# Decay image and constants of the fills: two and four transfers from SP's queue, in a rewritten order, in place of three and six from GpSimd's

## The chip, the core and the metric

The kernel runs on one core of a Trainium2 chip. Its engines work side by side, each on its own list of instructions in order: PE (matrix multiplication, with PEld for its weight loads), DVE (VectorE), ACT (ScalarE), POOL (GpSimd) and SP (SyncE, which here only issues transfers). The metric is device microseconds of one execution, the median of the runs. Times in the text are microseconds from the start of the profiled span unless they say otherwise.

## The reference

A causal attention with a decay ("forgetting") term, followed by a gated feed-forward block with a short convolution. Sizes: 8 batches, 8 heads, 576 positions, 64 columns per head; the feed-forward goes from 512 to 1024 and back.

```
scores = q @ k.T / sqrt(64)
cum    = cumsum(log(clip(f, 1e-4, 1)))            # per batch and head, along the sequence
scores = where(causal, scores + cum[i] - cum[j], -1e9)
x      = softmax(scores) @ v                      # heads side by side: [8, 576, 512]
h      = relu(x @ w_in)                           # [8, 576, 1024]
c      = conv along the sequence, 3 taps per column
out    = (h * sigmoid(c)) @ w_out                 # float32 [8, 576, 512]
```

## The kernel before

**Tiling.** The 64 pairs of batch and head are cut into 16 head blocks (hb) of four heads; two make a batch. The 576 positions are cut into five blocks of keys and queries (four of 128 and one of 64). For a block, q and k stand transposed in one SBUF tile `qk` (a ring of four): 64 rows of each head's data lie at the odd partitions, and the even partitions hold extra rows that the matmul of the scores sums over as well. The decay enters through three of them: on q's side one row holds cum scaled for the queries and two rows hold ones; on k's side one row holds -1 and two rows hold the scaled cum, split in two bf16 parts. Thus `cum[i] - cum[j]` is part of the product, and no other engine adds it.

**How the rows get there.** `kc` (128 x 576, bf16) is made by DVE from a running sum: partitions 0 to 63 the leading part of cum of the 64 heads, 64 to 127 the rest. It is written to a tensor in DRAM, `image`, of four rows (j), two sides (a: q, k), 64 heads and 576 positions; that is task `ki` (`decay_image`, lines 325 to 327). The constants of the image (the ones, the -1 and a zero row on both sides) and a tensor of zeros, `blank`, are written by task `zc` (`constants`, lines 329 to 332). From there three kinds of block read:

- Block 0 takes the decay by extra matmuls from `kc` directly (lines 364 and 366) and reads no image.
- Blocks 1 to 9 (`NCL` = 10) have q and k put in place with one DVE or ACT operation (`cl`) which also writes the constant rows (line 238 for blocks 2 to 9); then `rw` (`rows_of`, lines 254 and 255) brings the three varying rows from the image with two transfers.
- Blocks 10 to 15 are loaded by transfers alone: after the transposing loads, `fi` (`fill`, lines 246 and 248) brings 60 zero rows from `blank` and all four rows of both sides from the image. Only these blocks, heads 40 to 63, use the constants in the image.

**Stages of one head block**, by the names in the order: `q` (transposing load of q or k, line 232; blocks 0 and 1 have plain loads `ld`, line 211, and PE transposes `tp`, line 218, instead), `v` (loads of v, line 261), `va` (cast of v, lines 269 and 271), then per pair of heads `sd` (scores of the diagonal blocks, line 361), `so` (the blocks below it, line 361), per block `st` (the last 64 positions), with the exponentials `ed`, `eo`, `et` on ACT; blocks 0 to 5 mask by a matmul (line 369), the later ones on POOL (`md`, `mt`). Then `pv` (product with v, lines 443 and 447), `n` (division by the sum, line 457), `t` and `tx` (transposition, lines 464 to 474).

**Stages of one batch's feed-forward**, for eight column blocks ff: `f` (line 483, 0.98 us each when PE runs freely), `r` (relu, lines 495 and 497), `c` and `d` (the convolution, lines 502 and 504, DVE), `a` (tanh, line 507, ACT), `g` (gate, line 511, DVE), `k` (copies of the last 64 positions of two batches into one tile, line 516), `o` (line 522), `e` (copy of the result from PSUM) and `s` (store). In the last batch `o7.c.ff` is one matmul of chunk c; chunks 0 and 1 share one PSUM tile, 2 and 3 another, and chunk 4 has its own; their copies are `e7.c` (lines 532 and 537). The weights are loaded in quarters (`wi`, `wo`, line 570) and cast (`wic`, `woc`, line 578).

**What sets the order.** Nothing is scheduled at run time. The string `ORDER` lists every task once; `Plan.play` runs through it and emits each task's instructions, so an engine's list is the order of the tasks that are its own. `name@ENGINE` picks the engine for tasks that several could do. Buffers are handed out in the same order (a task that takes a buffer gets the one freed first), and an engine that comes to an instruction whose inputs or buffer aren't ready waits, with all that stands behind it. Waits are kept per tile: a matmul into one half of a PSUM tile waits for a copy from its other half that stands ahead of it in the order. SP's list therefore is one queue: a transfer that waits for its source holds up all loads behind it.

Of the kernel before, what the change touches and what calls it, by code (L numbers as in the profile page):

```python
# [17 lines left out]
cw dca dcl tb ld0 ld0.0.0 ld0.0.1 ld0.1.0 ld0.1.1 ld1 ld1.0.0 ld1.0.1 v0.0 q2.1 q2.0 wi3@SP cwt dcs dck tp0.0.0  # L18
cl0.0.0@ACT tp0.0.1 tp0.1.0 tp0.1.1 cl0.1.1@DVE cl0.0.1@ACT sd0 cl0.1.0@ACT tp1.0.0 tp1.0.1 tp1.1.0 ed0 cl1.0.0@ACT v0.4
v0.2 cl1.1.0@DVE cl1.0.1@DVE sd1 tp1.1.1 cl1.1.1@ACT ki@POOL st0 rw1 so1.1 so1.0 cl2.1 cl2.0 ed1 eo1.1 et0 eo1.0 so0.1  # L20
sd3 v0.3 v0.1 va1.0@DVE so0.0 wic3@POOL va0.0@POOL va0.1@DVE eo0.1 ed3 q3.1 q3.0 eo0.0 sd2 ed2 so3.0 so2.1 so2.0 eo3.0
eo2.1 pv0.0 st1 so3.1 va1.1@DVE et1 wi0@SP wic0@POOL eo2.0 pv0.1 eo3.1 pv1.0 cl3.1 n0.0 n0.1 rw2 t0 pv1.1 cl3.0 tx0@ACT
sd4 so4.0 wi1@SP rw3 q5.1 n1.0 n1.1 t1 tx1@DVE wi2@SP v1.0 sd5 so5.1 q5.0 ed4 eo4.0 wic1@DVE f0.0 r0.0@DVE c0.0 cl5.1
d0.0 eo5.1 ed5 sd6 q4.0 wic2@POOL f0.1 ed6 so4.1 r0.1@ACT c0.1 v1.2 v1.3 f0.2 f0.3 st3 h0 eo4.1 a0.0 g0.0 d0.1 r0.2@ACT
r0.3@ACT et3 c0.2 c0.3 cl5.0 rw5 v1.1 va2.0@POOL q4.1 so6.1 so5.0 eo5.0 so6.0 eo6.0 sd7 ed7 f0.4 r0.4@ACT zc a0.1 d0.2
c0.4 d0.4 g0.1 f0.5 r0.5@ACT c0.5 d0.3 so7.0 eo7.0 f0.6 st2 et2 eo6.1 v1.4 a0.4 wo2@SP r0.6@DVE sd11 so7.1 so11.0 d0.5
cl4.0 va2.1@POOL wo1@SP g0.4 va3.0@POOL va3.1@POOL ed11 eo7.1 eo11.0 sd10 so10.0 c0.6 eo10.0 f0.7 r0.7@ACT ed10 pv2.0
so11.1 wo3@SP cl4.1 n2.0 d0.6 eo11.1 rw4 a0.2 v2.0 q6.1 pv2.1 so10.1 eo10.1 a0.3 a0.5 a0.6 pv3.0 pv3.1 n2.1 t2 n3.0
tx2@DVE n3.1 c0.7 g0.6 g0.3 d0.7 g0.5 woc2@POOL woc1@POOL sd9 so9.0 t3 ed9 tx3@ACT eo9.0 f1.0 sd8 r1.0@ACT c1.0 a0.7
g0.2 q6.0 cl6.1 d1.0 g0.7 st4 wo0@SP cl6.0 v2.2 so8.1 ed8 et4 eo8.1 f1.1 r1.1@ACT st5 f1.2 v2.4 so9.1 r1.2@ACT f1.3 f1.4  # L30
h1 et5 f1.5 c1.2 v2.3 v2.1 c1.1 a1.0 r1.3@ACT so8.0 rw6 v3.0 v3.1 c1.3 woc0@ACT g1.0 r1.4@ACT woc3@POOL eo9.1 eo8.0 o0.0
d1.3 r1.5@ACT a1.3 d1.1 sd13 sd12 o0.1 ed12 va4.0@DVE c1.4 pv4.0 f1.6 q7.1 q7.0 va5.0@ACT e0.0@ACT va4.1@ACT g1.3 c1.5
d1.4 d1.2 d1.5 ed13 r1.6@ACT pv4.1 n4.0 n4.1 va5.1@ACT a1.5 so13.0 eo13.0 a1.4 a1.1 md13 v3.3 pv5.0 pv5.1 n5.0 n5.1
so12.1 f1.7 q9.1 q9.0 cl7.1 c1.6 g1.1 t4 eo12.1 tx4@ACT v3.2 t5 tx5@ACT r1.7@ACT a1.2 cl7.0 d1.6 a1.6 c1.7 o0.2 k0@POOL
o0.3 rw7 g1.4 g1.2 v3.4 d1.7 v4.0 md12 q8.0 q8.1 e0.1@ACT g1.6 cl9.0 st6 so13.1 et6 eo13.1 f2.0 r2.0@ACT f2.1 c2.0 g1.5
a1.7 r2.1@ACT s0.0@SP f2.2 r2.2@ACT sd15 c2.2 f2.3 so15.1 so12.0 d2.0 g1.7 va6.0@DVE ed15 cl9.1 va7.0@DVE va7.1@DVE c2.1
eo15.1 h2 r2.3@ACT f2.4 sd14 eo12.0 r2.4@ACT ed14 o1.0 a2.0 rw9 q10.1 q10.0 so14.0 st7 so14.1 cl8.0 d2.1 c2.3 g2.0 cl8.1
eo14.1 eo14.0 o1.1 e1.0@ACT va6.1@ACT pv6.0 et7 k1@ACT f2.5 mt7 mt6 r2.5@ACT sd18 pv6.1 n6.0 so15.0 d2.3 a2.1 n6.1
eo15.0 o1.4 md15 md14 ed18 st9 et9 so18.0 t6 d2.2 e1.2@DVE sd19 pv7.0 eo18.0 ed19 c2.4 g2.1 c2.5 tx6@ACT f2.6 so19.1
pv7.1 r2.6@ACT n7.0 n7.1 v4.1 eo19.1 f2.7 so18.1 a2.2 a2.3 eo18.1 rw8 mt9 d2.4 c2.6 md19 d2.5 g2.2 sd16 ed16 a2.5  # L40
r2.7@ACT md18 s0.1@SP d2.6 a2.6 a2.4 v4.2 md16 q11.1 o1.2 t7 tx7@DVE sd17 g2.3 o1.3 v4.4 f3.0 v4.3 ed17 g2.5 c2.7 q11.0
s1.0@SP d2.7 e1.1@ACT r3.0@ACT fi10 so17.0 eo17.0 so16.1 f3.1 r3.1@ACT a2.7 c3.0 g2.4 d3.0 g2.6 f3.2 h3 r3.2@ACT eo16.1
g2.7 f3.3 f3.4 md17 c3.1 r3.3@ACT so19.0 so16.0 r3.4@ACT eo19.0 va9.0@DVE va9.1@ACT eo16.0 so17.1 v5.0 s1.2@SP c3.2 d3.1
c3.3 a3.0 g3.0 fi11 o2.0 f3.5 d3.3 a3.1 eo17.1 st8 r3.5@ACT g3.1 c3.5 va8.0@DVE d3.5 d3.2 c3.4 o2.1 sd20 et8 e2.0@ACT
f3.6 sd21 so20.1 ed20 r3.6@ACT ed21 md21 pv8.0 md20 eo20.1 n8.0 so21.0 v5.3 pv9.0 eo21.0 so21.1 pv9.1 va8.1@POOL mt8
v5.2 q12.0 v5.4 v5.1 n9.0 n9.1 a3.3 g3.3 d3.4 eo21.1 sd23 ed23 md23 pv8.1 n8.1 q12.1 so23.1 eo23.1 f3.7 q13.1 s2.0@SP t9
fi12 r3.7@DVE c3.7 st10 t8 sd22 a3.5 et10 tx8@ACT o2.2 a3.4 ed22 c3.6 tx9@DVE f4.0 mt10 k2@POOL so20.0 o2.3 so22.0 g3.5
va10.0@ACT d3.7 eo20.0 a3.7 pv10.0 r4.0@DVE md22 c4.0 d3.6 a3.2 e2.1@ACT eo22.0 va11.0@DVE g3.4 n10.0 g3.7 a3.6 so22.1
f4.1 f4.2 f4.3 r4.2@ACT g3.6 c4.2 g3.2 d4.0 h4 r4.1@ACT d4.2 f4.4 c4.1 so23.0 r4.3@ACT eo22.1 eo23.0 r4.4@ACT o3.0 c4.3
a4.0 g4.0 d4.3 va10.1@POOL q13.0 st11 sd24 sd25 ed24 et11 ed25 o3.1 so25.0 st12 pv11.0 e3.0@ACT et12 mt12 c4.4  # L50
va11.1@ACT d4.1 d4.4 mt11 v6.0 pv10.1 f4.5 eo25.0 a4.3 r4.5@ACT a4.4 a4.1 a4.2 n11.0 n10.1 g4.3 s2.1@SP f4.6 pv11.1
n11.1 f4.7 g4.4 c4.5 d4.5 g4.1 k3@POOL r4.6@ACT r4.7@ACT t11 c4.6 md24 c4.7 so25.1 eo25.1 fi13 a4.5 v6.2 t10 tx10@ACT
tx11@ACT v6.1 v6.3 g4.5 va12.0@DVE g4.2 d4.6 d4.7 o3.2 st13 o3.3 e3.1@ACT sd27 et13 md25 q14.1 q14.0 f5.0 ed27 so27.0
eo27.0 a4.6 a4.7 r5.0@DVE v6.4 f5.1 r5.1@DVE f5.2 sd26 so26.1 ed26 eo26.1 f5.3 f5.4 c5.0 g4.6 g4.7 r5.2@DVE d5.0
r5.3@ACT v7.0 v7.3 c5.3 c5.2 va13.0@DVE va12.1@ACT so26.0 eo26.0 so24.0 o4.0 eo24.0 h5 so24.1 o3.4 a5.0 md27 eo24.1 d5.2
f5.5 r5.4@ACT a5.2 k4@ACT s3.1@SP fi14 q15.1 g5.0 d5.3 e3.2@ACT s1.1@SP v7.1 r5.5@ACT c5.1 c5.4 g5.2 d5.4 d5.1 c5.5 a5.3
g5.3 d5.5 f5.6 so27.1 eo27.1 sd28 mt13 q15.0 o4.1 r5.6@ACT ed28 st14 e4.0@ACT et14 pv12.0 sd29 v7.2 s3.2@SP pv12.1 md26
pv13.0 va13.1@DVE n12.0 n12.1 a5.1 ed29 mt14 md29 a5.4 n13.0 so28.0 pv13.1 n13.1 t12 f5.7 t13 a5.5 eo28.0 c5.6 r5.7@ACT
tx12@DVE tx13@DVE so28.1 g5.1 d5.6 so29.0 so29.1 eo28.1 eo29.1 a5.6 g5.5 c5.7 va15.0@DVE g5.6 g5.4 f6.0 f6.1 r6.0@ACT
f6.2 f6.3 v7.4 va15.1@ACT r6.1@ACT eo29.0 d5.7 c6.0 fi15 md28 sd31 o4.2 r6.3@ACT r6.2@ACT va14.0@POOL a5.7 ed31 sd30  # L60
so30.0 o4.3 st15 ed30 c6.3 eo30.0 c6.1 et15 d6.0 d6.3 c6.2 g5.7 d6.1 mt15 va14.1@POOL so30.1 h6 eo30.1 so31.1 eo31.1
e4.1@ACT pv14.0 f6.4 pv14.1 so31.0 n14.0 n14.1 md31 r6.4@ACT md30 f6.5 s3.0@SP a6.1 eo31.0 pv15.0 pv15.1 c6.4 d6.4 a6.0
a6.3 s4.1@SP n15.0 n15.1 a6.4 g6.4 g6.3 d6.2 r6.5@ACT f6.6 r6.6@ACT c6.6 c6.5 g6.1 d6.6 d6.5 o5.0 o5.1 f6.7 e5.0@ACT
r6.7@ACT c6.7 tx14 tx15 s4.0@SP s5.0@SP o5.2 k5@ACT a6.2 g6.2 g6.0 f7.0 f7.1 d6.7 r7.0@ACT a6.6 a6.7 f7.2 f7.3 g6.6 c7.0
g6.7 d7.0 r7.3@ACT o5.3 o5.4 r7.2@ACT c7.2 r7.1@ACT c7.1 a6.5 d7.1 c7.3 d7.2 h7 a7.0 g6.5 e5.2@ACT a7.1 e5.1@ACT g7.1
f7.4 f7.5 f7.6 r7.4@ACT a7.2 c7.4 g7.0 d7.3 o6.0 o6.1 o7.0.0 r7.6@ACT a7.3 r7.5@ACT e6.0@ACT g7.2 c7.6 c7.5 d7.4 a7.4
g7.3 d7.5 k6@ACT a7.5 f7.7 o6.2 g7.4 d7.6 s5.2@SP s5.1@SP k7.3@ACT s6.0@SP k7.0@DVE k7.4@DVE k7.1@POOL o7.0.1 o6.3
o7.2.0 r7.7@ACT c7.7 g7.5 o7.2.1 o7.2.2 o7.3.0 o7.3.1 o7.3.2 o7.1.0 o7.2.3 d7.7 e6.1@ACT a7.6 s6.1@SP g7.6 k7.6@DVE
o7.0.2 o7.2.4 o7.0.3 o7.2.5 o7.0.4 o7.1.1 o7.1.2 o7.3.3 o7.1.3 o7.1.4 o7.0.5 o7.0.6 a7.7 g7.7 o7.0.7 k7.2@ACT k7.5@ACT
k7.7@ACT e7.0@ACT o7.1.5 o7.1.6 o7.1.7 e7.1.1 s7.1.1 o7.3.4 s7.0@SP e7.1.0 s7.1.0 o7.4.0 o7.4.1 o7.4.2 o7.4.3 o7.4.4  # L70
o7.2.6 o7.2.7 e7.2@ACT s7.2@SP o7.4.5 o7.4.6 o7.4.7 e7.4@ACT o7.3.5 o7.3.6 o7.3.7 e7.3@ACT s7.4@SP s7.3@SP
# [691 lines left out]
```

## Time and profile before

| What | Value |
|---|---|
| Median of 3 runs | 249.28 us (249.09 to 250.06) |
| The profiled execution | 250.55 us, of which the span is 248.8 |
| Mean granted clock of TensorE | 0.991 |
| Busy: PE, DVE, ACT, POOL | 230.4, 217.0, 212.7, 58.1 us |
| Moved by transfers | 47.64 MB, mean 191 GB/s |
| POOL's transfers (software queue) | 0.73 MB in 304 packets |

The span runs from the first to the last instruction. A row of a timeline gives start, duration, engine, line and operation, how many instructions were merged, and in brackets the idle time ahead of it with what ended it. A row of the stretches gives the time of the stretch and its length, then for PE, PEld, DVE, ACT and POOL the busy time with the number of instructions, then the granted clock, the share of the 16 transfer engines that was busy (it can exceed 1) and GB/s. SPq and POOL rows with DMA are the issue of a transfer, not the transfer itself.

### The profile page before, as it was taken

Reading aid. Unit: us, or ns where it says so; the run is one execution under the profiler, and the core shown is the slowest. Engines: PE = TensorE matmul, PEld = TensorE weight load, DVE = VectorE, ACT = ScalarE, POOL = GpSimd, SP = SyncE. Lnnn points to the kernel's source line nnn. Section 1 sums busy time; section 2 is a strip of 40 time slices with the busy share of each in tenths; the row PEclk is TensorE's granted clock in tenths of the full one; section 3 lists DMA queues with packets and bytes.
Section 4 is the critical chain, followed back from the end, with each engine's and each line's share of the span. In section 5 each row is a group of like instructions: output and inputs, shape, how many; then the busy total and the mean of one; then the engine's idle time right before and its main releaser. Section 6 shows DMA issues by size and latency. Waiting matters only on the chain.

```text
span 248.8 us, 6462 instructions
## 1 busy us (share of the span) xinstructions
PE 230.4 (93%) x2644; PEld 146.7 (59%) x2644; DVE 217.0 (87%) x337; ACT 212.7 (85%) x288; POOL 58.1 (23%) x89
## 2 busy tenths in 40 slices
...
PEclk9999799999999999999999999999999999999998
...
GB/s 171 311 164 233 196 223 201 222 219 282 242 215 209 173 200 206 238 201 224 259 246 190 182 252 250 212 180 263 242 211 175 4 0 134 219 0 126 84 126 170
DMA packets 115899, 47.64 MB, mean 191 GB/s; under 512 B 106258, under 2 KB 106514, under 8 KB 115870
## 3 DMA queue, kind: packets, MB, share of 16 engines
...
q0 software_dynamic: 304, 0.73, 0.8%
q10 hardware_dynamic: 310, 0.42, 0.6%
q8 instruction: 20, 0.33, 0.5%
q14 instruction: 9, 0.07, 0.1%
HBM read 19.96 MB, written 10.17 MB: 121 GB/s over the span
## 4 chain that ended last, share of the span: by engine, by line
PE 74%; DMA 7%; DVE 6%; ACT 5%; SPq 4%; issue 2%; DVEq 0%; ACTq 0%
PE ps L522 24%; PE ps L483 19%; PE ps L361 14%; PE ps L443 7%; DMA qk<-image 5%; ACT pp L419 2%; PE ps L447 2%; DMA hg<-in_k_dram 2%; PE ps L218 2%; PE ps L464 2%; DVE u L502 2%; SPq L261 2%; DVE u L504 1%; PE ps L369 1%; PE ps L364 1%
## 5 line engine op out<-in xcount | busy, mean ns | idle before, releaser
L483 PE MATMUL ps<-xt,w_in_f 128*128 128x512 f16 (+1 forms) x512 | 69.4, 286 | 0.8 <-ACT xt L474 0.7
L419 ACT ACTIVATE pp<-ps 128x1024 f16<-128x1024 f32 x64 | 65.1, 1039 | 3.7 <-PE ps L366 2.3
L361 PE MATMUL ps<-qk 128*128 128x128 bf16 (+2 forms) x576 | 63.5, 242 | 4.8 <-DMA qk<-image 4.1
L522 PE MATMUL ps<-w_out_f,hg 128*128 128x512 f16 x256 | 59.6, 379 | 0.8 <-ACT ob L532 0.7
L504 DVE SCALAR_TENSOR_TENSOR u<-ht,cwt,u 128x576 f32<-128x576 f16 x64 | 55.2, 876 | 0.2
L361 PEld LDWEIGHTS <-qk 128*128 128x128 bf16 x576 | 38.8, 99 | 23.5 <-DMA qk<-image 4.8
L502 DVE SCALAR_TENSOR_TENSOR u<-ht,cwt 128x576 f32<-128x576 f16 x64 | 51.8, 825 | 0.7 <-ACT hg L507 0.3
L507 ACT ACTIVATE hg<-u,cw 128x576 f16<-128x576 f32 x64 | 48.7, 791 | 3.7 <-DVE u L504 3.6
L483 PEld LDWEIGHTS <-w_in_f 128*128 128x128 f16 x512 | 34.1, 98 | 29.5 <-issue 1.2
L511 DVE SCALAR_TENSOR_TENSOR hg<-hg,ht 128x576 f16<-128x576 f16 x64 | 49.0, 778 | 0.4 <-ACT hg L507 0.3
L495 ACT ACTIVATE ht<-ps 128x576 f16<-128x576 f32 x57 | 37.0, 671 | 5.3 <-DVE hg L511 2.9
L522 PEld LDWEIGHTS <-hg 128*128 128x128 f16 x256 | 24.0, 98 | 26.8 <-issue 1.3
L405 POOL TENSOR_SCALAR_AFFINE_SELECT pp<-pd 128x1024 f16<-128x1024 f32 x20 | 24.5, 1236 | 49.7 <-ACT pd L402 49.7
L457 DVE TENSOR_TENSOR xm<-ps,rc 128x896 f16<-128x896 f32 (+1 forms) x32 | 24.3, 758 | 1.2
L443 PE MATMUL ps<-va,pp 128*128 128x65 f16 x640 | 24.6, 193 | 0.1
L443 PEld LDWEIGHTS <-pp 128*128 128x128 f16 x640 | 22.7, 97 | 2.0
L402 ACT ACTIVATE pd<-ps 128x1024 f32<-128x1024 f32 x20 | 20.7, 1042 | 0.8 <-PE ps L361 0.8
L384 POOL TENSOR_SCALAR_AFFINE_SELECT pt<-p 128x256 f16<-128x256 f32 x10 | 5.5, 560 | 55.6 <-ACT p L381 55.6
L402 ACT ACTIVATE pp<-ps 128x1024 f16<-128x1024 f32 x12 | 12.2, 1021 | 6.4 <-PE ps L361 4.6
L528 ACT COPY ob<-ps 128x1024 f32<-128x1024 f32 (+1 forms) x16 | 15.5, 966 | 1.9 <-PE ps L522 1.9
L238 DVE TENSOR_SCALAR qk<-qk,lim 128x2304 uint16<-128x2304 uint16 x16 | 14.0, 874 | 3.3 <-DMA qk<-in_k_dram 2.5
L369 PE MATMUL ps<-mask,ident 128*128 128x512 bf16 (+1 forms) x30 | 11.2, 374 | 1.3 <-ACT pp L402 0.7
...
## 6 DMA issues: line engine op xcount, KB each, us to landing
...
```

The lines of the kernel that those rows point to most:

```text
L361: nc.tensor.matmul(o, tk[:, h * S + k0:h * S + k0 + 128], tq[:, h * S + q0:h * S + q0 + n], start=first, stop=last and not by_matmul(hb, h))
L402: nc.scalar.activation(o, ps_of(f"sd{i}").rearrange("p (s c) -> p s c", s=2), AF.Exp, scale=SCALE)
L405: nc.gpsimd.affine_select(pair(i)[:, :, 0:512].rearrange("p s (m j) -> p s m j", j=128), pd_t[slot[f"ed{i}", "pd"]].rearrange("p s (m j) - ...
L419: nc.scalar.activation(pair(i)[:, s, 512:1536], ps_of(f"so{i}.{s}"), AF.Exp, scale=SCALE)
L443: nc.tensor.matmul(ps[:, c:c + D + 1], block(hb, h, m, n), va[:, h, m, 0:D + 1], start=(m == 0), stop=(m == n))
L483: nc.tensor.matmul(ps[:, c:c + n], w_in_f16[:, cc, 128 * ff:128 * (ff + 1)], xt[:, cc // 2, x:x + n], start=(cc == 0), stop=(cc == NCC - 1))
L495: nc.scalar.activation(o, i, AF.Relu, scale=0.5)
L502: nc.vector.scalar_tensor_tensor(u, ht[:, 0:S], cwt[:, ff, 0:1], ht[:, 1:1 + S], op0=ALU.mult, op1=ALU.add)
L504: nc.vector.scalar_tensor_tensor(u, ht[:, 2:2 + S], cwt[:, ff, 1:2], u, op0=ALU.mult, op1=ALU.add)
L507: nc.scalar.activation(hg_of(b, ff), u_t[slot[f"c{b}.{ff}", "u"]], AF.Tanh, scale=cw[:, ff, 1:2])
L511: nc.vector.scalar_tensor_tensor(hv, hv, 1.0, ht_of(b, ff)[:, 1:1 + S], op0=ALU.add, op1=ALU.mult)
L522: nc.tensor.matmul(ps[:, 512 * (c % 2):512 * (c % 2 + 1)], w, w_out_f16[:, ff, :], start=(ff == 0), stop=(ff == NFF - 1))
```

## The change

- `image` is laid out with the side first, [2, 4, 64, 576] instead of [4, 2, 64, 576]; the readers are adapted and move the same bytes.
- `ki` writes with two transfers instead of three: q's row, and k's two rows at once from all 128 partitions of `kc`. It moves from POOL to SP.
- `zc` writes only heads 40 to 63, with three transfers (ones twice, -1, zeros twice) in place of five for all heads, and one for `blank` as before. It moves from POOL to SP.
- `ORDER` is another list throughout: the same tasks, in part in another order and, for some forty of them, on another engine among DVE, ACT and POOL.

```diff
-    image = dpool.tile([4, 2, BH, S], BF16, name="image")
+    image = dpool.tile([2, 4, BH, S], BF16, name="image")
...
-                          image[:, :, hb * HH:(hb + 1) * HH, :].rearrange("j a h s -> j a (h s)"))
+                          image[:, :, hb * HH:(hb + 1) * HH, :].rearrange("a j h s -> j a (h s)"))
...
-        nc.sync.dma_start(even_rows(hb, 0, 1, h0 * S, HS), image[0:1, 0, c, :].rearrange("j h s -> j (h s)"))
-        nc.sync.dma_start(even_rows(hb, 1, 2, HS + h0 * S, 2 * HS), image[1:3, 1, c, :].rearrange("j h s -> j (h s)"))
+        nc.sync.dma_start(even_rows(hb, 0, 1, h0 * S, HS), image[0, 0:1, c, :].rearrange("j h s -> j (h s)"))
+        nc.sync.dma_start(even_rows(hb, 1, 2, HS + h0 * S, 2 * HS), image[1, 1:3, c, :].rearrange("j h s -> j (h s)"))
...
     def decay_image(e):
-        for j, a, h in ((0, 0, 0), (1, 1, 0), (2, 1, 1)):
-            {"SP": nc.sync, "POOL": nc.gpsimd}[e].dma_start(image[j, a], kc[BH * h:BH * (h + 1)])
-
-    def constants():
-        for j, a, c in ((1, 0, plus), (2, 0, plus), (0, 1, minus), (3, 0, zero[:, 0:S]), (3, 1, zero[:, 0:S])):
-            nc.gpsimd.dma_start(image[j, a], c)
-        nc.gpsimd.dma_start(blank, zero[0:60])
-
+        queue(e).dma_start(image[0, 0], kc[0:BH])
+        queue(e).dma_start(image[1, 1:3].rearrange("j b s -> (j b) s"), kc)
+
+    def constants(e):
+        c0, n = HH * NCL, BH - HH * NCL
+        queue(e).dma_start(image[0, 1:3, c0:].rearrange("j b s -> b j s"), plus[0:n].unsqueeze(1).broadcast_to((n, 2, S)))
+        queue(e).dma_start(image[1, 0, c0:], minus[0:n])
+        queue(e).dma_start(image[:, 3, c0:].rearrange("a b s -> b a s"), zero[0:n, 0:S].unsqueeze(1).broadcast_to((n, 2, S)))
+        queue(e).dma_start(blank, zero[0:60])
...
-    add("zc", "POOL", [], constants)
+    add("zc", "SP/POOL", [], constants)
...
-    add("ki", "SP/POOL", ["dck"], decay_image)
+    add("ki", "SP/POOL/ACT", ["dck"], decay_image)
```

The order is cut here to the lists of single engines at the places that matter. First SP's list, from the start to rw7:

```diff
-ld0 ld0.0.0 ld0.0.1 ld0.1.0 ld0.1.1 ld1 ld1.0.0 ld1.0.1 v0.0 q2.1 q2.0 wi3 v0.4 v0.2 rw1 v0.3 v0.1 q3.1 q3.0 wi0 rw2 wi1
-rw3 q5.1 wi2 v1.0 q5.0 q4.0 v1.2 v1.3 rw5 v1.1 q4.1 v1.4 wo2 wo1 wo3 rw4 v2.0 q6.1 q6.0 wo0 v2.2 v2.4 v2.3 v2.1 rw6
-v3.0 v3.1 q7.1 q7.0 v3.3 q9.1 q9.0 v3.2 rw7
+ld0 ld0.0.1 ld0.0.0 ld0.1.0 ld1 ld0.1.1 ld1.0.0 ld1.0.1 v0.0 ki q2.0 q2.1 v0.4 v0.3 rw1 wi0 v0.2 v0.1 q3.0 q3.1 wi3 rw2 wi1
+rw3 q5.1 wi2 q5.0 v1.0 q4.1 v1.1 v1.3 rw5 v1.2 q4.0 v1.4 wo1 wo3 wo2 rw4 v2.0 q6.0 q6.1 v2.4 wo0 v2.2 v3.0 v3.2 rw6
+v2.1 v2.3 q7.1 v3.1 zc q7.0 q9.1 v3.3 q9.0 rw7
```

PE's list at the start, around the first use of rw7 (sd15, sd14), and at the end:

```diff
-cw tp0.0.0 tp0.0.1 tp0.1.0 tp0.1.1 sd0 tp1.0.0 tp1.0.1 tp1.1.0 sd1 tp1.1.1 st0 so1.1 so1.0 so0.1 sd3 so0.0 sd2 so3.0 so2.1 so2.0 pv0.0
+cw tp0.0.0 tp0.0.1 tp0.1.0 tp0.1.1 tp1.0.0 tp1.0.1 tp1.1.0 tp1.1.1 sd0 sd1 so1.0 so0.1 so1.1 sd2 sd3 so0.0 so2.0 st0 pv0.0
...
-so12.1 f1.7 t4 t5 o0.2 o0.3 st6 so13.1 f2.0 f2.1 f2.2 sd15 f2.3 so15.1 so12.0 f2.4 sd14
+t4 so13.1 t5 so13.0 o0.2 st6 o0.3 so12.0 so12.1 f2.0 f2.1 f2.2 f2.3 f2.4 sd15 sd14
...
-o7.0.6 o7.0.7 o7.1.5 o7.1.6 o7.1.7 o7.3.4 o7.4.0 o7.4.1 o7.4.2 o7.4.3 o7.4.4 o7.2.6 o7.2.7 o7.4.5 o7.4.6 o7.4.7 o7.3.5 o7.3.6 o7.3.7
+o7.1.5 o7.1.6 o7.1.7 o7.0.7 o7.2.3 o7.2.4 o7.2.5 o7.2.6 o7.2.7 o7.3.4 o7.3.5 o7.3.6 o7.3.7 o7.4.0 o7.4.1 o7.4.2 o7.4.3 o7.4.4 o7.4.5 o7.4.6 o7.4.7
```

POOL's list at the start:

```diff
-ki wic3 va0.0 wic0 wic2 va2.0 zc va2.1 va3.0 va3.1
+va0.1 wic0 wic3 wic2 va2.0 va2.1 va3.0 va3.1
```

In the last batch, `e7.0` stands ahead of o7.1.5 in the whole order before, and behind o7.0.7 after, and moves from ACT to DVE with `e7.3`.

109 lines of the change are left out of this document (55 added, 54 removed).

## The prediction

> **What bounds the kernel now.** I read the page first (shares, slices, granted clock), then the busy time by stretches, then the order of time on SP's queue, PE and GpSimd at the places that the change touches, and last the chain of waits at the end. The page:
>
> ```profile
> span 248.8 us, 6462 instructions
> PE 230.4 (93%) x2644; PEld 146.7 (59%) x2644; DVE 217.0 (87%) x337; ACT 212.7 (85%) x288; POOL 58.1 (23%) x89
> PEclk9999799999999999999999999999999999999998
> ```
>
> The busy time of each engine by stretches (PE, PEld, DVE, ACT, POOL; then clock, share of the DMA engines, GB/s):
>
> ```profile
> 0.00:10.00 10.00, 4.33 (x38) 4.02 (x39) 7.43 (x29) 5.59 (x5) 6.62 (x33) 1.00 0.75 225
> 20.00:30.00 10.00, 7.52 (x58) 4.89 (x57) 2.81 (x4) 5.39 (x7) 2.60 (x2) 0.83 1.19 214
> ...
> 50.00:60.00 10.00, 8.42 (x121) 5.72 (x119) 9.86 (x13) 10.00 (x14) 5.86 (x9) 1.00 1.01 226
> 60.00:70.00 10.00, 8.67 (x130) 6.03 (x129) 9.90 (x15) 8.06 (x11) 4.27 (x5) 1.00 1.29 259
> 70.00:80.00 10.00, 8.57 (x72) 4.79 (x72) 9.97 (x15) 9.24 (x15) 0.00 (x0) 1.00 1.07 220
> ...
> 100.00:120.00 20.00, 20.00 (x264) 13.33 (x263) 19.57 (x31) 19.71 (x28) 7.86 (x8) 1.00 1.13 220
> ...
> 240.00:250.00 10.00, 3.99 (x17) 1.55 (x16) 0.42 (x1) 2.52 (x5) 0.00 (x0) 0.88 0.40 132
> ```
>
> PE is idle for 248.8 - 230.4 = 18.4 us in all, and nearly all of that lies in the first 80 us and the last ten: 5.7 in the first ten, 2.5 between 20 and 30, then 1.6 + 1.3 + 1.4 = 4.3 between 50 and 80, where VectorE is busy 9.9 of 10, and 4.8 after 240. In between (100 to 120 stands for it) PE is busy throughout, with VectorE at 98%. So no change of order gains anything from about 80 to 240; what it can win or lose is decided in the first 80 us, in waits newly made later, and in the tail. GpSimd, at 23%, isn't the bound.
>
> **ki, the decay image.** SP's queue at the start, and two instructions of GpSimd's:
>
> ```profile
> 5.99 7.56 SPq L232 DMA_TRANSPOSE qk<-in_k_dram  x1
> 13.60 4.71 SPq L232 DMA_TRANSPOSE qk<-in_q_dram  x1
> 18.36 0.58 SPq L570 DMA_DIRECT2D ob<-in_moe_w_in_dram  x1
> 18.99 1.36 SPq L261 DMA_DIRECT2D vf<-in_v_dram  x2
> 20.53 0.33 SPq L254 DMA_DIRECT2D qk<-image  x1
> ...
> 80.78 3.19 SPq L232 DMA_TRANSPOSE qk<-in_q_dram  x1
> ```
>
> ```profile
> 9.03 1.75 POOL L327 DMA_DIRECT2D image<-kc  x3 [2.27 <-DVE kc L321]
> ```
>
> GpSimd loses three issues, 1.75 us, at a time when it only waits. SP gains two; its issues here take 0.58 (L570) to 0.68 (1.36 for two), so 1.2 us, and they can't begin before kc is there at 9.03. Queued behind that new wait on SP are both transposes of head block 2 (q2.0, q2.1), v0.4, v0.3 and rw1, and PE waits for rw1. The first transpose moves from 5.99 to about 9.03 + 1.2 = 10.2, that is 4.2 later. But before, its issue took 7.56 where one at 80.78 took 3.19: for 4.4 us it stood behind the loads ahead of it, and the new wait fits into that. I take 0 as its cost; the bounds are 0 and 4.2. That the image lands sooner wins nothing: SP reached rw1 only at 20.53, after a transpose and three loads, not after a wait for the image.
>
> What helps is another move in the same stretch of SP's order: weight load wi3 (18.36) goes behind rw1, to after the transposes of block 3, and wi0 now comes right after rw1. PE's side, and the landing of rw1 in the chain of waits:
>
> ```profile
> 16.86 0.27 PE L369 MATMUL ps<-mask,ident 128*128 128x256 bf16 x1
> ...
> 18.22 0.19 PE L361 MATMUL ps<-qk 128*128 128x64 bf16 x1
> ...
> 22.15 0.38 PE L369 MATMUL ps<-mask,ident 128*128 128x512 bf16 x1
> 25.01 0.40 PE L361 MATMUL ps<-qk 128*128 128x128 bf16 x4 [2.48 <-DMA qk<-image]
> ```
>
> ```profile
> 21.04 3.92 DMA qk<-image
> ```
>
> The rows of the image land at 21.04 + 3.92 = 24.96 and PE goes on at 25.01, after 2.48 us of nothing. Without wi3 ahead the issue comes 18.99 - 18.36 = 0.6 earlier and 512 KB less are queued ahead of it, 2.4 us at the 214 GB/s of this stretch. I take 2.4 (the bytes, which the issue overlaps), so a landing at 22.5; bounds 3.0 early and, with the transposes 4.2 late, 3.6 late (28.6). PE's order changes with it: st0 (16.86 to 18.22, 1.36 us) comes after sd2 and sd3, not ahead, so PE is ready for the rows 1.36 sooner but has that much more left. The gain is 25.01 - 22.5 - 1.36 = 1.15 us. On top, the clock in 20:30 is 0.83 on average: 0.17 x 10 = 1.7 us lost in the stretch that holds the wait of 2.48. PE would now wait from 22.53 - 1.36 = 21.2 to 22.5, 1.3 us, and the 1.4 us of smaller waits in 70:80 left the clock at 1.00, so I count the 1.7 as won: 2.85 together, bounds +3.4 and, at 28.6, -4.95.
>
> [...]
>
> Not all of 2.85 reaches the end: from 50 to 80 PE is held by VectorE (9.86 to 9.97 of 10) and by rows that come at the pace of DMA engines whose share is 1.0 or over. I take half, **1.4**; bounds 0 and 2.85.
>
> One thing goes the other way at once: k's plain load of the first pair is now issued ahead of q's, while PE turns q first.
>
> ```profile
> 6.01 1.14 PE L218 MATMUL ps<-ident_b,hg 128*128 128x128 bf16 x9 [0.48 <-DMA hg<-in_q_dram]
> 7.79 3.06 PE L218 MATMUL ps<-ident_b,hg 128*128 128x128 bf16 x27 [0.64 <-DMA hg<-in_k_dram]
> ```
>
> The nine transposes at 6.01 move to 7.8 or so: up to 1.14 us, hidden in the 1.3 of waiting that is left, so 0; if the rows come sooner than I think it costs 1.1 of that.
>
> **zc, the constants.** GpSimd before, with the cast behind them and PE's wait for it:
>
> ```profile
> 55.12 2.08 POOL L331 DMA_DIRECT2D image<-signs  x3
> 57.19 1.04 POOL L331 DMA_DIRECT2D image<-zero  x2
> 58.22 0.70 POOL L332 DMA_DIRECT2D blank<-zero  x1
> 58.91 0.41 POOL L271 CAST va<-vf 64x256 f16<-64x256 f32 x1
> ```
>
> ```profile
> 59.37 0.22 PE L447 MATMUL ps<-va,pt 128*64 128x65 f16 x2 [0.51 <-POOL va L271]
> ```
>
> 3.8 us of issuing go from GpSimd, the cast of V (va2.1) starts that much sooner, and PE's 0.51 goes. What is late next there is VectorE, so I take **0.3** (0 to 0.5). On SP come four issues, 4 x 0.6 = 2.4 us, and 5 x 27 + 135 = 270 KB (24 of the 64 rows), 1.2 us at the 220 GB/s of 70:80; together up to 3.6, between q7.1 and q7.0. Behind them on SP stand q7.0, q9.1, v3.3, q9.0 and rw7; the issue of rw7, and PE's work up to its first use:
>
> ```profile
> 93.17 0.36 SPq L254 DMA_DIRECT2D qk<-image  x1
> 93.59 0.59 SPq L255 DMA_DIRECT2D qk<-image  x1
> ```
>
> ```profile
> 92.59 3.10 PE L483 MATMUL ps<-xt,w_in_f 128*128 128x512 f16 x24
> 95.76 0.61 PE L361 MATMUL ps<-qk 128*128 128x128 bf16 x8
> ```
>
> PE uses the rows at 95.76, two us after their issue and without a wait: there is no slack in the old order. The new one puts f2.3, f2.4 (1.0 each, from 3.10 for three) and so12.0 ahead of sd15, over 2.0 us. So up to 3.6 - 2.0 = 1.6 could show, less what SP is early by; I take a loss of **0.5**, bounds 0 and 3.6. The fills that need the constants begin after 120 us (slices of a full PE), so their landing costs nothing.
>
> **The tail.** In order of time, on PE and in the chain of waits:
>
> ```profile
> 240.44 1.02 PE L522 MATMUL ps<-w_out_f,hg 128*128 128x512 f16 x4 [0.72 <-ACT ob L532]
> ```
>
> ```profile
> 239.81 0.59 ACT ob L532
> 240.44 2.55 PE ps L522 x11
> 243.06 0.59 ACT ob L532
> 243.69 0.82 PE ps L522 x3
> 244.54 0.58 ACT ob L532
> ```
>
> PE waits 0.72 for ScalarE's copy of chunk 0, because the copy stands in the order before the last three matmuls into the other half of the same PSUM tile (o7.1.5 to o7.1.7). The new order has all matmuls of a tile ahead of its copies, and o7.4 (its own tile) last. I take **0.7**; bounds 0 and 0.9. The last store becomes two of 128 KB on two queues for one of 256: 0.
>
> **About thirty other operations** change between VectorE, ScalarE and GpSimd (relus, casts of V, tails), both ways; each is 0.4 to 1.0 us and none stands on the path that sets the end outside 50 to 80. I take 0, bounds 1 either way.
>
> **Sum.** 1.4 + 0.3 - 0.5 + 0.7 = 1.9 us. The profiled execution took 250.55 (span 248.8 and 1.75 around it), 1.27 over the median of the runs, 249.28. So 248.65 for a profiled one, and for the median 249.28 - 1.9 = **247.4**.
>
> **Rivals.** (a) Slower: the wait for kc on SP isn't hidden, and the transposes of block 2, and rw1 behind them, come 4.2 late. From a landing after 25.01 - 1.36 = 23.65 the step loses; at 28.6 it loses 4.95, half of which reaches the end: 249.28 + 2.5 - 0.5 = 251.3. For it: SP issues in order, and the new wait lies at the head of the queue. Against: the 4.4 us that the first transpose stood anyway. (b) The early gain is all used up between 50 and 95 by VectorE and SP: 249.28 - 0.3 + 0.5 - 0.7 = 248.8. For it: 9.9 of 10. Against: VectorE has only 2.8 of 10 in 20:30, so it too can start sooner. (c) zc on SP delays rw7 by its full 3.6: 247.4 + 3.1 = 250.5. For it: no slack at 95.76. Against: the later place of sd15. [...] (d) All 2.85 is kept: 247.4 - 1.45 = 245.9. (e) The clock drops in 20:30 whatever the wait is: the early step is 1.15, half of it 0.6, and the time 249.28 - 0.6 - 0.5 = 248.2. For it: only one wait of this size stands in the trace to read the price from. Against: the clock is 1.00 in every stretch of shorter waits.
>
> **Chances.** Forecast 0.43, (a) 0.20, (b) 0.15, (c) 0.08, (d) 0.07, (e) 0.07. About 0.5%, 1.25 us, is what can be told from no change: 248.03 to 250.53. Faster: 0.41 of the forecast, 0.07 of (d), 0.03 each of (b) and (e): 0.54. Same: 0.12 of (b), 0.04 of (e), 0.02 of the forecast, 0.05 of (c): 0.23. Slower: (a) and 0.03 of (c): 0.23. The likeliest case alone spans 246 to 248.4. To hold 8 in 10 the range reaches past (d) on one side and to (a) on the other: 245.0 to 251.4.
>
> **What would show it.** Right: rw1 landing near 22.5, the wait at 25.01 under 1.5 us and the clock in 20:30 near 1.00; GpSimd's cast va2.1 straight after va2.0; no wait of PE for the image around 95; no wait of 0.7 at 240. Wrong: q2's transposes landing over 2 us later than before, PE idle in 20:30 above 3 us; a wait for rw7 or rw4 of more than a microsecond; PE idle in 50:80 above 4.3 by as much as the early gain.

## The result and the profile after

The changed kernel takes 246.62 us (median of four runs, 246.26 to 251.2) against 249.67 (the three runs above and one of 252.22); the ratio of the runs is 0.9875, 95% interval 0.983 to 0.9921. Some executions take over 1.5% longer than the fastest of their kernel (here 251.2); the medians count them, the ratios and the clocks of the runs leave them out. Run again beside the mixed orders below it was 0.9886 (0.9842 to 0.9929). So it is faster by 1.2%, some 3 us; the forecast was 1.9 less, 247.4, in the range 245.0 to 251.4.

The page of the changed kernel's profiled execution (246.97 us):

```profile
span 245.1 us, 6460 instructions
PE 229.3 (94%) x2644; PEld 147.4 (60%) x2644; DVE 215.4 (88%) x334; ACT 211.1 (86%) x284; POOL 62.2 (25%) x87
PEclk9999999999999999999999999999999999999999
```

Its busy time by stretches, with the columns of the prediction's table:

```profile
0.00:10.00 10.00, 4.94 (x44) 4.60 (x44) 7.99 (x30) 4.56 (x4) 5.56 (x31) 1.00 0.76 252
10.00:20.00 10.00, 9.24 (x103) 7.86 (x101) 4.51 (x4) 7.18 (x6) 0.00 (x0) 1.00 1.14 203
20.00:30.00 10.00, 9.98 (x142) 7.45 (x141) 3.21 (x6) 7.80 (x10) 1.43 (x2) 1.00 1.06 226
30.00:40.00 10.00, 9.26 (x143) 6.87 (x142) 7.29 (x14) 6.61 (x9) 1.04 (x1) 1.00 0.87 228
40.00:50.00 10.00, 8.48 (x78) 5.01 (x77) 9.03 (x12) 9.03 (x12) 1.32 (x1) 1.00 1.02 211
50.00:60.00 10.00, 9.08 (x148) 6.45 (x147) 9.86 (x13) 9.88 (x14) 4.92 (x5) 1.00 0.93 259
60.00:70.00 10.00, 8.29 (x111) 5.54 (x108) 9.90 (x16) 8.65 (x12) 3.66 (x3) 1.00 0.98 210
70.00:80.00 10.00, 9.64 (x79) 5.33 (x78) 10.00 (x15) 10.00 (x15) 0.58 (x1) 1.00 0.94 197
```

Two stretches of the kernel before that the prediction doesn't show:

```profile
30.00:40.00 10.00, 9.59 (x188) 7.72 (x186) 6.73 (x12) 7.98 (x10) 1.10 (x1) 1.00 0.84 203
40.00:50.00 10.00, 9.95 (x92) 5.99 (x91) 8.76 (x12) 9.90 (x14) 1.65 (x1) 1.00 1.07 220
```

And the end of PE's work in the changed kernel, then ScalarE's last copy:

```profile
226.37 12.25 PE L524 MATMUL ps<-w_out_f,hg 128*128 128x512 f16 x56
238.46 1.89 PE L524 MATMUL ps<-w_out_f,tl 128*128 128x512 f16 x8
```

```profile
240.43 0.59 ACT L534 COPY ob<-ps 128x512 f32<-128x512 f32 x1 [1.19 <-PE ps L524]
```

PE's last matmul ends at 238.46 + 1.89 = 240.35, before at 243.69 + 0.81 = 244.50. The span therefore splits like this:

| Part of the span, us | Before | After | Difference |
|---|---|---|---|
| PE idle up to its last matmul (end less busy) | 14.1 | 11.05 | -3.05 |
| PE busy (the same 2644 matmuls) | 230.4 | 229.3 | -1.1 |
| From the last matmul to the end | 4.3 | 4.75 | +0.45 |
| Span | 248.8 | 245.1 | -3.7 |

These are two single executions; the medians differ by 3.05. Where the clock is lower before (0.83 in 20:30, 1.00 after) matmuls are longer (one of mask and ident, 128x512, takes 0.38 at 22.15, with the clock at 1.00 in that microsecond, and 0.63 at 28.24, with 0.50), but the busy time doesn't go by the clock alone: a second profile of the changed kernel (after_again) has 227.8, and it too has a clock of 1.00 in every stretch up to PE's last matmul. Of the idle time, 20:30 lost 2.46 and 70:80 1.1, but 40:50 has 1.5 more and 10:20 0.8. In all, PE is idle for 13.0 us before 80 in the one and 11.1 in the other. How far PE has come with its work is another matter: the first matmul of o0.0 starts at 75.91 before and at 75.45 after, only 0.46 us earlier. The second group of experiments takes this up.

SP's queue in the changed kernel, at the start and at the constants:

```profile
8.66 0.47 SPq L327 DMA_DIRECT2D image<-kc  x1
9.45 0.34 SPq L328 DMA_DIRECT2D image<-kc  x1
9.84 3.72 SPq L233 DMA_TRANSPOSE qk<-in_q_dram  x1
13.61 3.69 SPq L233 DMA_TRANSPOSE qk<-in_k_dram  x1
...
18.90 0.34 SPq L255 DMA_DIRECT2D qk<-image  x1
...
79.58 0.33 SPq L332 DMA_DIRECT2D image<-signs  x1
...
91.05 0.38 SPq L255 DMA_DIRECT2D qk<-image  x1
```

The first transpose starts 3.85 us later than before (9.84 against 5.99) and yet the pair is through at 17.30, a microsecond earlier than at 18.31. rw1 is issued at 18.90 in place of 20.53, and PE goes from the work ahead of it straight into sd2, without a wait. The constants' four issues take 1.6 us from 79.58, and rw7 is issued at 91.05, before at 93.17.

### The profile page after: what moved, and what is told of

The parts are those of the page before. It is cut to its first block, busy times and chain, and to the rows that moved or that the text cites. A ratio compares the mean times of both kernels' runs of the same rounds, so it can differ in the third digit from the quotient of the medians.

```text
span 245.1 us, 6460 instructions
## 1 busy us (share of the span) xinstructions
PE 229.3 (94%) x2644; PEld 147.4 (60%) x2644; DVE 215.4 (88%) x334; ACT 211.1 (86%) x284; POOL 62.2 (25%) x87
## 4 chain that ended last, share of the span: by engine, by line
PE 74%; DVE 12%; ACT 4%; issue 3%; SPq 3%; DMA 2%; POOL 0%; DVEq 0%; ACTq 0%; POOLq 0%
PE ps L524 25%; PE ps L485 21%; PE ps L363 13%; PE ps L445 6%; DMA qk<-in_k_dram 2%; PE ps L466 2%; PE ps L449 2%; SPq L233 2%; DVE u L506 2%; DVE qk L239 2%; PE ps L219 2%; DVE u L504 2%; ACT ht L497 1%; DVE xm L459 1%; DVE ht L499 1%
## 5 line engine op out<-in xcount | busy, mean ns | idle before, releaser
L363 PE MATMUL ps<-qk 128*128 128x128 bf16 (+2 forms) x576 | 62.6, 240 | 0.3 <-DVE xm L459 0.3
L524 PE MATMUL ps<-w_out_f,hg 128*128 128x512 f16 x256 | 59.0, 379 | 0.2 <-ACT w_out_f L580 0.2
L506 DVE SCALAR_TENSOR_TENSOR u<-ht,cwt,u 128x576 f32<-128x576 f16 x64 | 52.6, 839 | 1.0 <-DVE u L504 0.5
L509 ACT ACTIVATE hg<-u,cw 128x576 f16<-128x576 f32 x64 | 49.3, 791 | 3.5 <-DVE u L506 3.3
L445 PE MATMUL ps<-va,pp 128*128 128x65 f16 x640 | 23.9, 193 | 0.8 <-POOL va L270 0.7
L239 DVE TENSOR_SCALAR qk<-qk,lim 128x2304 uint16<-128x2304 uint16 x16 | 15.9, 996 | 4.7 <-DMA qk<-in_k_dram 4.7
L386 POOL TENSOR_SCALAR_AFFINE_SELECT pt<-p 128x256 f16<-128x256 f32 x10 | 8.9, 886 | 37.2 <-ACT p L383 37.2
L530 ACT COPY ob<-ps 128x1024 f32<-128x1024 f32 (+1 forms) x17 | 16.1, 950 | 1.9 <-PE ps L524 1.9
L518 POOL COPY tl<-hg 128x64 f16<-128x64 f16 (+1 forms) x8 | 4.6, 610 | 31.0 <-DVE hg L513 31.0
```

The lines of the kernel that those rows point to most:

```text
L363: nc.tensor.matmul(o, tk[:, h * S + k0:h * S + k0 + 128], tq[:, h * S + q0:h * S + q0 + n], start=first, stop=last and not by_matmul(hb, h))
L445: nc.tensor.matmul(ps[:, c:c + D + 1], block(hb, h, m, n), va[:, h, m, 0:D + 1], start=(m == 0), stop=(m == n))
L506: nc.vector.scalar_tensor_tensor(u, ht[:, 2:2 + S], cwt[:, ff, 1:2], u, op0=ALU.mult, op1=ALU.add)
L509: nc.scalar.activation(hg_of(b, ff), u_t[slot[f"c{b}.{ff}", "u"]], AF.Tanh, scale=cw[:, ff, 1:2])
L524: nc.tensor.matmul(ps[:, 512 * (c % 2):512 * (c % 2 + 1)], w, w_out_f16[:, ff, :], start=(ff == 0), stop=(ff == NFF - 1))
```

## The experiments

All were timed against the kernel before on the chip where they ran; three groups of four, each group on one chip. Ratios of different groups are therefore compared across chips. "Clock" is the mean of the granted clock over the runs in the ratio; for the kernel before it is 0.988, 0.992 and 0.991 in the three groups. It is a mean over the whole span, and in many of these profiles the clock also falls behind PE's last matmul, where nothing is lost: in the changed kernel's it is 0.60 and 0.50 in the microseconds from 244 to 246, PE's last matmul having ended at 240.35, and new_ki_pool's has a mean of 0.994 with 1.00 from 0 to 120 and from 220 to 240 and 0.76 in 240:250, PE's last matmul having ended at 239.38.

| Run | What it is | Median, us | Runs in the ratio | Ratio (95% interval) | Clock |
|---|---|---|---|---|---|
| the change | | 246.62 | 3 of 4 | 0.9875 (0.983 to 0.9921) | 0.998 |
| q_pool | change, both transfers on GpSimd | 245.3 | 6 of 6 | 0.9824 (0.9782 to 0.9866) | 0.998 |
| old_order_q_sp | old order, both on SP | 248.37 | 11 of 12 | 0.9942 (0.9908 to 0.9976) | 0.994 |
| old_wi3_late | before, wi3 behind rw1 | 249.35 | 8 of 12 | 0.9958 (0.9923 to 0.9993) | 0.993 |
| new_wi0_early | change, wi0 ahead of rw1 | 246.81 | 5 of 6 | 0.9847 (0.9795 to 0.9898) | 0.995 |
| after_again | the change | 246.59 | 6 of 6 | 0.9886 (0.9842 to 0.9929) | 0.993 |
| new_to_tx1 | new order to 36 us, then old | 250.44 | 7 of 12 | 0.9972 (0.9927 to 1.0017) | 0.993 |
| new_to_o00 | new order to 75 us, then old | 248.17 | 12 of 12 | 0.9959 (0.9928 to 0.999) | 0.997 |
| old_to_o00 | old order to 75 us, then new | 247.04 | 5 of 6 | 0.9885 (0.9845 to 0.9925) | 0.992 |
| before_new_tail | before, last 12 us in the new order | 250.96 | 12 of 12 | 1.0025 (0.9988 to 1.0061) | 0.989 |
| old_new_transfers | before, transfers rewritten only | 249.41 | 12 of 12 | 1.0008 (0.997 to 1.0045) | 0.989 |
| new_ki_pool | change, image on GpSimd | 245.42 | 6 of 6 | 0.981 (0.9762 to 0.9859) | 0.996 |
| new_zc_pool | change, constants on GpSimd | 246.57 | 5 of 6 | 0.984 (0.9789 to 0.9891) | 0.998 |

### First group: is it the one load, or the queue?

My theory was the prediction's: a weight load less ahead of rw1. The rival: the transfers' new queue.

**q_pool**

```diff
-ki@SP ... zc@SP
+ki@POOL ... zc@POOL
```

> The changed kernel with its order, but decay image and constants issued from GpSimd's queue (two and four transfers) at the same places of the order. My theory (the gain is the order of the first 30 us, above all that no weight load stands ahead of rw1): 246.2 to 247.2, no wait of PE for the image, clock in 20:30 at 0.99 or more; SP's first transpose starts at about 5.3 in place of 9.8. Rival (the gain is the move of the transfers to SP): back to 248.5 or more.

Its queue at the start:

```profile
6.02 6.89 SPq L232 DMA_TRANSPOSE qk<-in_q_dram  x1
...
17.21 0.34 SPq L254 DMA_DIRECT2D qk<-image  x1
```

The time is 245.3, under the 246.2 to 247.2 that my theory gave: with the new order the move to SP is not the gain. Without the wait for kc at its head, SP issues rw1 at 17.21, 1.7 us ahead of the changed kernel.

**old_order_q_sp**

```diff
-v0.0 q2.1 q2.0 wi3@SP cwt dcs dck ... ki@POOL
+v0.0 cwt dcs dck ki@SP q2.1 q2.0 wi3@SP
...
-q7.0 ... zc (on POOL, near 55 us)
+zc@SP q7.0
```

> The order of before, with only the transfers of decay image and constants rewritten and moved to SP: the image right ahead of block 2's transposes, the constants between q7.1 and q7.0. My theory: no gain, 248.6 to 250.2, the wait of 2.5 us for the image at 25 and the clock of 0.83 in 20:30 stay; rw7 comes up to 2 us later, with a wait there. Rival (the move is the gain): 247 or less.

PE's waits of over 1.5 us, and one stretch:

```profile
23.38 0.40 PE L362 MATMUL ps<-qk 128*128 128x128 bf16 x4 [2.30 <-DMA qk<-image]
...
51.46 0.38 PE L362 MATMUL ps<-qk 128*128 128x128 bf16 x4 [2.45 <-DMA qk<-image]
...
94.35 0.61 PE L362 MATMUL ps<-qk 128*128 128x128 bf16 x8 [1.59 <-DVE u L503]
```

```profile
20.00:30.00 10.00, 7.27 (x99) 5.29 (x97) 2.55 (x4) 7.10 (x9) 2.60 (x2) 1.00 1.26 208
```

A gain of 0.6%, where my theory had none. Two of the waits are those that it named: 2.30 for rw1, and 1.59 at the first use of rw7. The profile puts the second down to a VectorE instruction that ended just then, but that one writes `u`, which these matmuls don't read. They do read the rows, issued at 91.54 and 91.96; PE goes on 2.4 us after the later issue, and 2.1 after it in new_to_o00 below (91.40 and 93.46), where the profile names the rows. So it was likely the rows; the trace doesn't show their landing. The wait of 2.45 near 51 is new. And the clock stayed at 1.00 through waits of 2.30 and 2.45.

**old_wi3_late**

```diff
-q2.1 q2.0 wi3@SP ... rw1 ... q3.1 q3.0 wi0@SP
+q2.1 q2.0 ... rw1 ... q3.1 q3.0 wi3@SP wi0@SP
```

> The kernel before with one load moved: weight load wi3 from ahead of rw1 to behind the transposes of block 3 (and its cast ahead of wi0's). My theory: rw1 lands at 22 to 23 in place of 25, PE's wait in 20:30 is under 1 us, the clock there 0.97 or more, and the time 247.0 to 248.2 (1 to 2.3 us less). Rival (the order of the other tasks is what counts): 248.8 or more, with the wait shortened but given back by 80.

```profile
21.48 0.40 PE L361 MATMUL ps<-qk 128*128 128x128 bf16 x4 [0.48 <-DMA qk<-image]
...
33.80 0.40 PE L361 MATMUL ps<-qk 128*128 128x128 bf16 x4 [1.58 <-DMA qk<-image]
...
52.29 0.38 PE L361 MATMUL ps<-qk 128*128 128x128 bf16 x4 [2.54 <-DMA qk<-image]
```

The step works as worked out: the rows land by 21.48, and the wait falls from 2.48 to 0.48. But the time falls by only 0.4%, and by the medians of all runs (249.35 against 250.07) by 0.3%. PE meets the next waits sooner: 1.58 for a later block's rows at 33.80, where there was none, and 2.54 near 52, where there was 0.43.

**new_wi0_early**

```diff
-rw1 wi0@SP
+wi0@SP v0.4 ... rw1
```

> The changed kernel with one load moved back: weight load wi0 from right behind rw1 to ahead of v0.4, so that 512 KB stand ahead of rw1 again. My theory: rw1 lands 2 to 3 us later, PE waits 1 to 2.5 us for it at 23 to 25, the clock falls, and the time is 248.0 to 249.5. Rival: the wait is absorbed later, 246.2 to 247.2.

```profile
23.31 0.40 PE L362 MATMUL ps<-qk 128*128 128x128 bf16 x4 [1.00 <-DMA qk<-image]
...
53.07 0.40 PE L362 MATMUL ps<-qk 128*128 128x128 bf16 x4 [2.23 <-DMA qk<-image]
```

PE waits again, 1.00, and 2.23 near 53, but the clock doesn't fall, and the time stays where it was (0.9847, its interval overlapping that of the change). With this my theory in its simple form falls: the load ahead of rw1 decides the wait at 25, but not the time.

### Second group: in which part of the order is it?

The two orders were joined at one task: all tasks of the one up to it, then the rest as the other has them, with the transfers on SP in every case. The theory "early" puts the gain into the first stretch; "spread" says that each part of the old order has a wait of its own, and that what one part wins the next takes back.

```diff
+order = new order up to and with tx1 (or o0.0) + the remaining tasks in the old order
+order = old order up to and with o0.0 + the remaining tasks in the new order
```

> The changed kernel once more, so that the mixed orders beside it are compared on one chip. All theories: 246 to 247.2, ratio 0.983 to 0.992. It also says whether its profile has the clock of 1.00 in 20:30 again.

> The new order up to tx1 (the end of head blocks 0 and 1, some 36 us), then the rest of the tasks in the order of before, with the transfers on SP as in old_order_q_sp. Theory early (the gain is made in the first 36 us and kept): within 0.6 of after_again. Theory spread (the early gain is used up by waits for rw4 and rw7 in the old order, and the new order's later part is needed to keep it): 1 us or more above after_again, about the time of old_order_q_sp (248.4), with waits for the image of 2 us near 52 and 1.5 us near 94.

> The new order up to o0.0 (some 75 us), then the rest in the order of before. Theory early: within 0.6 of after_again but for the 0.7 of the old tail. Theory spread: no wait at 52, but the one for rw7 near 94 (1 to 1.6 us) and the old tail's 0.7: 1.5 to 2.3 above after_again.

> The order of before up to o0.0 with the transfers on SP, then the new order. Theory early: 248 or more, as old_order_q_sp. Theory spread: the wait near 52 stays, the one for rw7 and the tail's 0.7 go: 0.5 to 1.5 above after_again, 1 to 2 below old_order_q_sp.

new_to_tx1, one wait and one stretch:

```profile
60.05 2.38 PE L444 MATMUL ps<-va,pp 128*128 128x65 f16 x40 [2.88 <-DVE xm L458]
```

```profile
60.00:70.00 10.00, 9.23 (x128) 7.29 (x129) 8.86 (x15) 6.33 (x9) 1.64 (x2) 0.83 1.07 235
```

new_to_o00, PE at the first use of rw7 and in the tail:

```profile
93.46 0.61 PE L362 MATMUL ps<-qk 128*128 128x128 bf16 x8 [0.40 <-DMA qk<-image]
...
237.71 1.02 PE L523 MATMUL ps<-w_out_f,hg 128*128 128x512 f16 x4 [0.72 <-ACT ob L533]
```

old_to_o00, PE and one stretch:

```profile
23.94 0.40 PE L362 MATMUL ps<-qk 128*128 128x128 bf16 x4 [1.92 <-DMA qk<-image]
...
52.06 0.38 PE L362 MATMUL ps<-qk 128*128 128x128 bf16 x4 [2.51 <-DMA qk<-image]
```

```profile
50.00:60.00 10.00, 7.94 (x106) 5.69 (x107) 7.47 (x10) 7.06 (x9) 5.62 (x6) 0.83 1.07 272
```

after_again came out as expected (246.59, clock 1.00 in 20:30). "Early" falls: the new order up to 36 or 75 us with the old one behind it (0.9972, 0.9959) is no better than the old order throughout with the same queues (0.9942, on another chip), while the old order to 75 us with the new one behind it (0.9885) is as fast as the change, although it has waits of 1.92 and 2.51 and a clock of 0.83 once. "Spread" holds in part: the early 36 us alone end in a wait of 2.88 for VectorE at 60, with the clock down behind it. Its other waits came smaller: in new_to_tx1 0.71 near 50 and 0.16 near 94 in place of 2 and 1.5, in new_to_o00 the tail's 0.72 but 0.40 for rw7 in place of 1 to 1.6.

What neither theory said is that the part behind o0.0 carries the gain. In every trace the first matmul of o0.0 and PE's last one can be read; here they are for new_to_o00 and then for after_again, which have the same order up to o0.0:

```profile
73.83 1.89 PE L523 MATMUL ps<-w_out_f,hg 128*128 128x512 f16 x8 [0.16 <-ACT w_out_f L579]
240.96 0.81 PE L523 MATMUL ps<-w_out_f,hg 128*128 128x512 f16 x3
```

```profile
73.35 1.89 PE L523 MATMUL ps<-w_out_f,hg 128*128 128x512 f16 x8 [0.68 <-ACT w_out_f L579]
236.98 1.89 PE L523 MATMUL ps<-w_out_f,tl 128*128 128x512 f16 x8
```

| Profile | Order up to o0.0 | Order behind it | o0.0 starts | PE's last matmul ends | Between, us | PE idle in it |
|---|---|---|---|---|---|---|
| new_to_o00 | new | old | 73.83 | 241.77 | 167.94 | 1.82 |
| after_again | new | new | 73.35 | 238.87 | 165.52 | 0.36 |
| old_order_q_sp | old | old | 73.64 | 242.43 | 168.79 | 2.48 |
| old_to_o00 | old | new | 74.06 | 239.77 | 165.71 | 0.01 |
| before | old | old | 75.91 | 244.50 | 168.59 | 1.89 |
| the change | new | new | 75.45 | 240.35 | 164.90 | 0.01 |

Within the first two pairs the beginning is the same, and the new part behind o0.0 is 2.4 and 3.1 us shorter, 1.5 and 2.5 of it in waits; 0.4 to 0.5 is given back after PE's last matmul. All seven profiles with the old order there, before_new_tail counted among them, have 167.0 to 168.8 us between the two matmuls, all seven with the new one 164.9 to 165.7, and the clock is 1.00 in every stretch of that part up to 240 that the views cover. (Of PE's tasks one each differs between the two beginnings, st5 and f1.6.) The start of o0.0 scatters more, from 73.6 to 77.2 with the old beginning and from 72.6 to 75.5 with the new one, so a gain of up to a microsecond there can't be told. The pairs have the transfers on SP.

### Third group: the tail, the transfers' size, and each queue by itself

**before_new_tail**

```diff
+order = before up to and with f7.7 + the remaining tasks in the new order
```

> The kernel before up to f7.7, then the tasks in the new order (the last 12 us). My theory: PE's wait of 0.72 at the end is gone, the drain after PE's last matmul is 0.4 longer (two stores in place of one), 0.3 to 0.8 us in all: ratio 0.996 to 0.999. Rival (the tail is most of the gain behind o0.0): 1.5 us, ratio 0.994 or less.

```profile
238.81 1.06 PE L522 MATMUL ps<-w_out_f,hg 128*128 128x512 f16 x3 [0.59 <-DVE hg L511]
240.19 3.21 PE L522 MATMUL ps<-w_out_f,hg 128*128 128x512 f16 x14 [0.32 <-DVE hg L511]
```

No gain (1.0025). The wait of 0.72 for the copy is gone, but PE now waits 0.59 and 0.32 for VectorE's last gates: in the new order the matmuls that need them come earlier, and VectorE, which comes out of the old order here, isn't ahead enough, as I read it. In the whole new order there is no such wait (226.37 to 240.35 without a gap).

**old_new_transfers**

```diff
-order and code of before
+order of before, GpSimd's queue, ki with two transfers and zc with four for heads 40 to 63
```

> The order and the queues of before, only the transfers rewritten (two and four from GpSimd in place of three and six, 24 heads in place of 64). If the 0.6% that old_order_q_sp won comes from fewer bytes and issues: ratio 0.992 to 0.996. [...]

```profile
23.53 0.53 PE L362 MATMUL ps<-qk 128*128 128x128 bf16 x4 [2.06 <-DMA qk<-image]
...
61.68 2.38 PE L444 MATMUL ps<-va,pp 128*128 128x65 f16 x40 [3.49 <-DVE xm L458]
```

```profile
20.00:30.00 10.00, 7.94 (x75) 5.23 (x72) 2.50 (x4) 5.68 (x6) 2.60 (x2) 0.83 1.23 210
...
60.00:70.00 10.00, 7.61 (x116) 6.27 (x117) 9.43 (x16) 5.86 (x9) 2.15 (x2) 0.83 0.88 202
```

Fewer issues and bytes alone win nothing (1.0008). So the 0.6% of old_order_q_sp, measured on another chip, seems to belong to the move: to the image landing by SP's queue, to the transposes of block 2 that come behind it, or to GpSimd, which no longer issues the constants. Which of them isn't settled.

**new_ki_pool, new_zc_pool**

```diff
-ki@SP
+ki@POOL
```

```diff
-zc@SP
+zc@POOL
```

> The changed kernel with the image alone back on GpSimd, the constants on SP. If SP's wait for kc at the head of its queue is what cost the changed kernel against q_pool: SP's first transpose starts near 6.0, rw1 is issued near 17.3 and the ratio is 0.981 to 0.985. If not: 0.987 to 0.991.

> The changed kernel with the constants alone back on GpSimd, the image on SP. If the 1.6 us of issues between q7.1 and q7.0 cost anything in the new order: 0.981 to 0.985. If the later place of sd15 hides them: 0.987 to 0.991, as the changed kernel.

SP's queue in new_ki_pool:

```profile
6.73 6.41 SPq L232 DMA_TRANSPOSE qk<-in_q_dram  x1
...
17.89 0.35 SPq L254 DMA_DIRECT2D qk<-image  x1
```

With the image back on GpSimd rw1 is issued a microsecond sooner (17.89), and the ratio is 0.981; with both back it was 0.9824. Both figures lie 0.5 to 0.8% under the change's own 0.9875 and 0.9886, and their intervals overlap with its: it is likely, not shown, that the change would be better without its move of the image to SP. For the constants (0.984) nothing can be told.

## Why the prediction was right, and where not

The direction and the size came out, 3 us where 1.9 was forecast and the range held it. That was in good part luck: the largest term, the early 1.4, isn't where most of the time came from, and the part of the order that carries the gain was taken to be worth nothing but the tail's 0.7.

- **The wait for kc on SP** (taken as 0, bounds 0 and 4.2): right in the changed kernel's order. The first transpose starts 3.85 later and takes 3.72 in place of 7.56. Rival (a) didn't come about. A cost of 0 may be a little low, though: without the wait rw1 would have been issued up to 1.7 us earlier (17.21 in q_pool), and whether that costs time is left open above. The issues were dearer in the estimate than they are: 0.47 and 0.34, not 0.6 each.
- **rw1 without a weight load ahead of it** (2.85, half of it kept): the mechanism is there. In old_wi3_late the rows are there by 21.48, a microsecond earlier than worked out, and the wait at 25 goes. But its worth was not 1.4 by itself: 0.4% of 250 is 1.0 us (0.2 to 1.9) when done alone, and undoing it in the changed kernel cost nothing that could be measured. Nor did keeping the whole old beginning (old_to_o00, 0.9885). The step that failed is "I take half": no row stood behind that share, and the term was set down as one of its own, while the rows of the next blocks (33.80, 52.29) take back most of what this one wins.
- **The clock**: the price of 1.7 us after the wait was read from one execution, and at its place it is right, but it doesn't last. old_order_q_sp and old_to_o00 have the same list for PE up to o0.0; the first has no fall of the clock, the second has one behind 52.06:

```profile
54.37 1.14 PE L484 MATMUL ps<-xt,w_in_f 128*128 128x512 f16 x8
...
59.48 1.41 PE L444 MATMUL ps<-va,pp 128*128 128x65 f16 x40 [1.22 <-DVE xm L458]
```

```profile
56.57 1.14 PE L484 MATMUL ps<-xt,w_in_f 128*128 128x512 f16 x8
...
60.24 1.42 PE L444 MATMUL ps<-va,pp 128*128 128x65 f16 x40
```

  At the wait for the rows the second was 0.6 behind (52.06 against 51.46), after the fall 2.2 (56.57 against 54.37), and at the next wait for VectorE 0.76 (60.24 against 59.48): PE without the fall had to wait there. So most of what this fall cost was taken back in the stretch that VectorE holds. Rival (e), that the clock falls whatever the wait, is out: in the change, after_again, q_pool and new_to_o00 no wait of PE behind the first ten us is longer than 1.56, and the clock is 1.00 in every stretch up to 240.
- **zc on SP** (a loss of 0.5, bounds 0 and 3.6): the new order shows none, and rival (c) was, as far as that wait is the rows', a real cost in the old order, 1.59 at 94.35. What hides it is the later place of sd15, as worked out (PE comes to it at 95.90, 4.4 us after the rows' last issue), and SP, which reaches rw7 2.1 us sooner all the same; the issues take 1.6 us, not 2.4.
- **The cast of V behind zc** (0.3): the wait that it priced, for va2.1 at 59.37, is gone, but PE now waits 0.69 for the cast ahead of that one, va2.0, and nothing is won. Nor does va2.1 follow va2.0 at once, as the prediction's sign had it: it waits 1.61 for its load.

```profile
54.64 1.15 PE L445 MATMUL ps<-va,pp 128*128 128x65 f16 x32 [0.69 <-POOL va L270]
...
56.20 0.74 POOL L272 CAST va<-vf 64x256 f16<-64x256 f32 x1 [1.61 <-DMA vf<-in_v_dram]
```

- **The tail** (0.7): mis-sized. The wait of 0.72 is gone, the last stretch is 0.45 longer with its two stores, and alone the new tail gives nothing. VectorE's gates, which I left out, are the second condition.
- **"No change of order gains anything from about 80 to 240"**: this step failed. A PE that is busy throughout needn't be at its shortest: the part behind o0.0 became 2.4 and 3.1 us shorter in the two pairs, and 1.0 and 0.6 of that is PE's busy time (166.1 to 165.2, 166.3 to 165.7) at a clock of 1.00. The rest is waits, the tail's 0.72 among them. The "about thirty" operations on other engines, put at 0, are 39.
- **Rival (b)**, the early gain used up between 50 and 95, is what the partial changes did (old_wi3_late, new_to_tx1), and with o0.0 starting only 0.46 us earlier the changed kernel looks no different. Its time of 248.8 was wrong because the gain came from behind o0.0.

So what makes it faster, as far as the runs show, is the order behind o0.0: not the smaller transfers (1.0008), not their queue once the order is new (q_pool), and not the order of the first 75 us, with or without its one long wait (old_to_o00, new_to_o00). Fewer falls of the clock aren't it either: old_to_o00 has the gain with a mean clock of 0.992, that of the kernel before on the same chip, and new_to_o00 has 0.997 without it. Behind o0.0 PE waits less and is busy for less time; the new tail by itself gives nothing. Which of the moves there are needed isn't settled.
